# Four plain units instead of eight, another order of the first blocks, and two pairs of heads side by side in a fused retention and PReLU kernel

## The chip, the cores and the metric

The kernel runs on one core of a Trainium2 chip. The metric is the device time of one execution in microseconds (us). The engines are named as in the profile: PE does the matmuls and PEld loads their weights; DVE, ACT and POOL are the vector, scalar and GpSimd engines; SP issues most DMAs, and ACT issues some.

## The reference

Float32 retention over 8 batches, 8 heads, 576 positions and head size 64, followed by a feed-forward layer with a learned PReLU slope:

```python
scores = (1 / sqrt(64)) * q @ k^T
D[i, j] = gamma[h] ** (i - j) if i >= j else 0     # gamma[h] = 1 - 2 ** (-5 - h)
x = ((scores * D) @ v).transpose(0, 2, 1, 3).reshape(4608, 512)
h = x @ w_in                                        # 512 -> 2048
out = (max(h, 0) + alpha * min(h, 0)) @ w_out       # 2048 -> 512
```

The weights arrive in 8-byte floating point, so they are converted on the chip.

## The kernel before

**Retention.** For batches 1 to 7 the unit of work is a pair of heads, numbered `4 * batch + c`; pairs 4 to 7 are batch 1. Each sequence is cut into nine chunks of 64 positions. `load_kq` and `load_v` load a pair: q and k in a layout of 128-byte runs (tiles `qx`, `kx`, eight transfers of 72 KB), k again by rows (`kn`), and v (`vn`). `operands` scales q on POOL and turns `kx` and `qx` on DVE into `kT` and `qT`. `joint(n)` first makes the values of pair n-1 (matmul at line 758), whose copies go to the block tiles `x`; then, for pair n, the scores (L804, L796), the chunks' states (L813), the masked scores in `at`, and a recurrence over the chunks that leaves the running sums in `su`. Two DMAs carry `su` into `vn` and two carry `qT` into `at`, so the values are one product per chunk. For pairs 4 to 7 (`FIRST`) the masks run on ACT and POOL instead of DVE, and part of the loads is issued by ACT. Batch 0 is computed by position instead, in three parts of 256, 256 and 64 positions for all heads (`load_part`, `part_transposes`, `part_scores`, `part_states`, `part_values`, `last_part`), so that the first blocks have their x early.

**Feed-forward.** The 4608 positions form 18 blocks of 256, and the 2048 hidden features eight units of 256. A cell is one block with one unit. Blocks 0 and 1 lie in batch 0; block 2 needs batch 0 and batch 1; block 3 needs batch 1; block 4 also needs batch 2. The weights of a unit are four pieces of 128 x 1024 values: two of `w_in` and two of `w_out`. `convert` makes a piece float32 (two steps on ACT, three on DVE, one on POOL); `split_w` splits a piece into three parts of fewer bits (one step each on ACT, POOL and DVE), and `split_x` does it for a block's x.

A *split* unit (`unit`, then `split_g` and `second`) multiplies such parts: 24 matmuls at L1015 and 12 at L1064. A *plain* unit (`unit_plain`, `second_plain`; L951, L981) multiplies in plain float32 and needs only the converted weights and the unsplit x. Before, the first eight cells are plain: block 0 with units 0 and 1, block 1 with units 0 to 3, block 0 with units 2 and 3. All others are split.

**Order of blocks.** `order` lists visits: a block and the units done in it. A visit accumulates its units in PSUM and writes its sum to `o_kept` (or, at the end, to the output); a later visit of the same block loads that sum as `op` and adds to it. Blocks 0 to 13 are visited with units 0 to 3, blocks 14 to 17 in short visits while the other half of the weights replaces the first, then blocks 0 to 13 with units 4 to 7. `fetch_x` writes a block's x to memory at its first visit and reads it back at later ones. `todo` says after which cells the `joint` of a later pair is put, and `ahead` where the late weights are converted.

**PSUM.** There are eight banks: `psh` 2 (first products, values), `pso` 4 (second products), `psa` 2 (scores, states).

**The planner.** The code first records operations with an engine, an assumed cost, and what they read and write. `plan` derives each operation's urgency in a pass from the last operation backward, then fills the engines forward in time, the most urgent ready operation first. The result is a fixed order on each engine. SP and ACT issue DMAs in that order too, and an instruction that must wait holds up all that is behind it on its engine. `dma` (L218 to L220) records a transfer of any kind; all transfers therefore have line L220.

Functions that the change touches, with the profile's line numbers:

Of the kernel before, what the change touches and what calls it, by code (L numbers as in the profile page):

```python
# [21 lines left out]
def kernel(  # L22
# [195 lines left out]
    def dma(to, fro, size, r, w, eng="SP"):  # L218
        queue = {"SP": nc.sync, "ACT": nc.scalar}[eng]
        do(eng, 0.56, lambda: queue.dma_start(to(), fro()), r, w, late=size / RATE)  # L220
# [103 lines left out]
    LAG, FIRST = 2, range(4, 8)  # L324
# [296 lines left out]
    def convert(raw, wa, to, c=None):  # L621
# [33 lines left out]
        if to is None:  # L655
            tg, t0 = a, 0
        else:
            tg, t0 = to
# [4 lines left out]
            op1=ALU.bitwise_or), raws + [ck], [key] + ([ck] if to is None else []), lock=lock)  # L663
# [11 lines left out]
    plain = {}  # L675
# [23 lines left out]

    def load_kq(n):  # L700
        b, c = pairs[n]
        kx, qx, kn = Gen(kxs), Gen(qxs), Gen(kns[n % 2])
        loaded[n] = kx, qx, kn, vnm[n % 2]
        for g, src in ((qx, q), (kx, k)):
            for a in range(4):
                f0 = (a % 2) * 32
                dma(lambda g=g, a=a: g.get().rearrange("p (n r) -> p n r", r=32)[
                        32 * a:32 * a + 32],
                    lambda src=src, a=a, f0=f0: src[b, 2 * c + a // 2].rearrange(
                        "(n t) d -> t n d", t=32)[:, :, f0:f0 + 32], S * P, (), [(g, a)],  # L710
                    "ACT" if n in FIRST and g is qx else "SP")
# [12 lines left out]
    def operands(n):  # L724
# [3 lines left out]
        def f():  # L728
            qh = qx.get().rearrange("p (j x r) -> p j x r", x=2, r=32)
# [3 lines left out]
        four = [(qx, a) for a in range(4)]  # L733
        do("POOL", 1.15, f, (), four, lock=True)
        kT, qT = turned[n] = Gen(kTs[n % 2]), Gen(qTs[n % 2])
        for to, fro in ((kT, kx), (qT, qx)):
            do("DVE", 0.77, lambda to=to, fro=fro: nc.vector.transpose(to.get(), fro.get()),
               [(fro, a) for a in range(4)], [(to, 0)])
# [9 lines left out]
    def values(n, pv):  # L748
# [5 lines left out]
        for i, js in enumerate((range(0, j1), range(j1, NJ))):  # L754
            def f(i=i, js=js):
                for j in js:
                    for h2 in range(2):
                        nc.tensor.matmul(pv[i].get()[half(h2), (j - js[0]) * C:(j - js[0] + 1) * C],  # L758
                                         vns[n % 2][:, h2, j], mt.get()[:, h2, j], start=True,
# [18 lines left out]
    def joint(n):  # L778
# [10 lines left out]
        ps = [Gen(psa[p2]) for p2 in range(2)]  # L789
# [27 lines left out]
        mt = mts[n] = Gen(ats)  # L817
        for h2 in range(2):
            dma(lambda h2=h2: mt.get()[half(h2), h2].rearrange("p j s -> p (j s)"),
                lambda h2=h2: qT.get()[half(h2)], S * D * 4, [(qT, 0)], [(mt, "q", h2)])  # L820

        def masks(p2):
            for h2 in range(2):
                if n in FIRST:
                    def f(h2=h2):
                        to, x, h = half(1 - h2), half((1 - h2, h2)[p2]), 2 * c + h2
                        nc.scalar.activation(mt.get()[to, h2, p2:NJ - 1:2], at(p2)[x, 0],
# [3 lines left out]
                    def f(h2=h2):  # L831
                        t = mt.get()[half(1 - h2), h2, p2:NJ - 1:2]
# [7 lines left out]
        def masked(p2, h2):  # L840
            to, x, h = half(1 - h2), half((1 - h2, h2)[p2]), 2 * c + h2
            nc.vector.scalar_tensor_tensor(  # L842
                out=mt.get()[to, h2, p2:NJ - 1:2], in0=at(p2)[x, 0], scalar=pf[x, 1, h:h + 1],
                in1=mask[x, None, :].to_broadcast([C, NM - 1, C]), op0=ALU.mult, op1=ALU.mult)
        masks(0)
        for h2 in range(2):
            def f(h2=h2):
                to, h = half(1 - h2), 2 * c + h2
                nc.vector.scalar_tensor_tensor(
                    out=mt.get()[to, h2, NJ - 1], in0=pv[1].get()[to, 7 * C:],  # L850
                    scalar=pf[to, 1, h:h + 1], in1=mask[to], op0=ALU.mult, op1=ALU.mult)
            do("DVE", 0.285, f, [(pv[1], "x")], [(mt, "x", h2)])
        su = Gen(sus)
        g1, g2 = gch[:, 0, c:c + 1], gch[:, 1, c:c + 1]
        do("ACT", 0.37, lambda: nc.scalar.copy(su.get()[:, 0::2], at(0)[:, 1]), [(ps[0], 1)],
           [(su, "e")])
        for h2 in range(2):
            def f(h2=h2):
                x, y = half(h2), half(1 - h2)
                nc.vector.scalar_tensor_tensor(  # L860
                    out=at(0)[x, 0], in0=su.get()[x, 0::2], scalar=g1[x], in1=at(1)[y, 1],
# [3 lines left out]
        do("ACT", 0.22, lambda: nc.scalar.copy(su.get()[:, 1], at(0)[:, 0, 0]), [(ps[0], 0)],  # L865
           [(su, 1)])
        for j in range(3, NJ - 1, 2):
            do("DVE", 0.285, lambda j=j: nc.vector.scalar_tensor_tensor(
                out=su.get()[:, j], in0=su.get()[:, j - 2], scalar=g2, in1=at(0)[:, 0, j // 2],
                op0=ALU.mult, op1=ALU.add), [(su, j - 2), (ps[0], 0)], [(su, j)])  # L870
        do("DVE", 0.42, lambda: nc.vector.scalar_tensor_tensor(
            out=su.get()[:, 2::2], in0=su.get()[:, 1:NJ - 3:2], scalar=g1, in1=at(0)[:, 1, 1:],
            op0=ALU.mult, op1=ALU.add), [(su, 1), (su, 3), (su, 5), (ps[0], 1)], [(su, "e")])
        for h2 in range(2):
            dma(lambda h2=h2: vns[n % 2][half(h2), h2, 1:],
                lambda h2=h2: su.get()[half(h2)], (S - C) * D * 4,
# [3 lines left out]
    order = [(0, (0, 1)), (1, (0, 1, 2, 3)), (0, (2, 3))]  # L880
    order += [(kb, (0, 1, 2, 3)) for kb in range(2, 14)]
# [16 lines left out]
    def fetch_x(vis):  # L898
# [5 lines left out]
        else:  # L904
            x = Gen(xs[taken[0] % 2])
# [5 lines left out]
    def split_x(vis):  # L911
        x = vis["from"]
# [55 lines left out]
    def second_plain(cell):  # L968
        vis, u, ga = cell["vis"], cell["u"], cell["ga"]
        kb = vis["kb"]  # L970
        if cell["first"]:
            acc[:] = [Gen(pso[2 * (vis["n"] % 2) + m]) for m in range(2)]
# [123 lines left out]
    spare = Gen(lxs[1])  # L1096
# [4 lines left out]
    def weights(n):  # L1101
        for _ in range(n):
# [3 lines left out]
            elif at in (12, 14):  # L1106
                homes[0] = Gen(gs[at // 2 % 2])
# [162 lines left out]
```

## Time and profile before

| | |
|---|---|
| median of 3 runs (lowest, highest) | 980.65 us (980.06, 981.99) |
| the profiled execution's own time | 980.06 us |
| its span, first to last instruction | 978.3 us |
| mean granted TensorE clock | 0.984 |
| PE busy | 938.9 us, 96% of the span |
| PEld busy | 822.9 us, 84% |
| DVE, ACT, POOL busy | 615.4, 583.8, 638.1 us |
| moved by DMA | 134.93 MB, mean 138 GB/s |
| DMA packets | 255053, of them 218448 under 512 B |

Busy times are unions of the instructions' spans on an engine. Matmuls overlap in a pipeline, so a product's cost is best read from the distance between the starts of two groups. The granted clock is the share of full TensorE speed in a stretch. In a timeline a line gives the start, the duration, the engine, the line of code, the operation, its tiles and a count; in brackets, the idle time before it and what ended that. `SPq` is SP's instruction queue. DMA share is the mean busy share of 16 engines; packets in several queues at a time can bring it above 1.

### The profile page before, as it was taken

Reading aid. Unit: us, or ns where it says so; the run is one execution under the profiler, and the core shown is the slowest. Engines: PE = TensorE matmul, PEld = TensorE weight load, DVE = VectorE, ACT = ScalarE, POOL = GpSimd, SP = SyncE. Lnnn points to the kernel's source line nnn. Section 1 sums busy time; section 2 is a strip of 40 time slices with the busy share of each in tenths; the row PEclk is TensorE's granted clock in tenths of the full one; section 3 lists DMA queues with packets and bytes.
Section 4 is the critical chain, followed back from the end, with each engine's and each line's share of the span. In section 5 each row is a group of like instructions: output and inputs, shape, how many; then the busy total and the mean of one; then the engine's idle time right before and its main releaser. Section 6 shows DMA issues by size and latency. Waiting matters only on the chain.

```text
span 978.3 us, 22758 instructions
## 1 busy us (share of the span) xinstructions
PE 938.9 (96%) x8713; PEld 822.9 (84%) x8713; DVE 615.4 (63%) x1294; ACT 583.8 (60%) x1313; POOL 638.1 (65%) x515
## 2 busy tenths in 40 slices
PE   4897789999999999999999999999999999999998
PEld 3664578888998888888889899999999999999996
DVE  4777766778676777787667777654454445444444
ACT  2574455757666657575677676665555555555542
POOL 3666665766875857567688889765555555665553
PEclk9899889999999999999999999999999999999999
DMA  9989797788775879887533525242222222221111
GB/s 234 201 152 237 145 210 148 200 185 195 183 150 130 204 151 219 185 199 200 175 130 130 172 98 188 95 150 66 65 76 73 90 65 66 65 87 44 44 45 65
DMA packets 255053, 134.93 MB, mean 138 GB/s; under 512 B 218448, under 2 KB 218464, under 8 KB 254944
## 3 DMA queue, kind: packets, MB, share of 16 engines
q1 hardware_dynamic: 238624, 130.59, 52.5%
q10 hardware_dynamic: 16320, 2.89, 2.1%
q8 instruction: 68, 1.11, 0.5%
q14 instruction: 41, 0.34, 0.1%
HBM read 82.19 MB, written 35.65 MB: 120 GB/s over the span
## 4 chain that ended last, share of the span: by engine, by line
PE 85%; DMA 6%; DVE 3%; POOL 2%; issue 2%; ACT 1%; SPq 1%; ACTq 0%; POOLq 0%; DVEq 0%
PE psh L1015 38%; PE pso L1064 36%; PE psh L758 3%; PE psh L951 2%; DMA kn<-in_k_dram 2%; PE psa L804 1%; PE pso L981 1%; PE psa L813 1%; DMA vn<-su 1%; DMA w<-in_q_dram 1%; SPq L220 1%; DMA kx<-in_k_dram 1%; DMA op<-in_moe_w_in_dram 1%; DMA w<-in_moe_w_out_dram 1%; DVE at L842 0%
## 5 line engine op out<-in xcount | busy, mean ns | idle before, releaser
L1015 PEld LDWEIGHTS psh<-lx,w 128*128 128x128 f32 x3264 | 410.6, 192 | 14.0 <-DVE ga L1030 2.0
L1015 PE MATMUL psh<-lx,w 128*128 128x256 f32 x3264 | 420.0, 284 | 0.4 <-DVE ga L1030 0.3
L1064 PE MATMUL pso<-w,g 128*128 128x512 f32 x1632 | 402.8, 393 | 1.0 <-POOL g L1046 1.0
L1064 PEld LDWEIGHTS pso<-w,g 128*128 128x128 f32 x1632 | 295.8, 188 | 57.9 <-POOL g L1046 2.1
L1043 POOL TENSOR_TENSOR g<-ga,g 128x512 fp32r<-128x512 f32 x136 | 180.4, 1327 | 234.0 <-ACT g L1039 233.7
L1024 DVE SCALAR_TENSOR_TENSOR ga<-psh,gt 128x256 f32<-128x256 f32 x272 | 114.6, 422 | 175.8 <-ACT gt L1023 170.3
L1046 POOL TENSOR_TENSOR g<-g 128x512 fp32r<-128x512 f32 x136 | 178.5, 1312 | 12.0 <-ACT g L1041 2.0
L1030 DVE SCALAR_TENSOR_TENSOR ga<-psh,malpha,ga 128x256 f32<-128x256 f32 x272 | 130.2, 480 | 67.9 <-ACT psh L1027 66.9
L1027 ACT ACTIVATE psh<-ga 128x256 f32<-128x256 f32 x272 | 105.2, 388 | 88.3 <-DVE ga L1024 87.3
L1039 ACT ACTIVATE g<-ga 128x512 fp32r<-128x512 f32 x136 | 85.8, 631 | 119.8 <-PE pso L1064 105.9
L1023 ACT COPY gt<-psh 128x256 f32<-128x256 f32 x272 | 101.0, 371 | 67.6 <-PE psh L1015 59.6
L934 POOL TENSOR_TENSOR lx<-lx 128x512 fp32r<-128x512 f32 x78 | 102.4, 1322 | 18.8 <-DVE lx L924 16.2
L1041 ACT ACTIVATE g<-ga 128x512 fp32r<-128x512 f32 x136 | 84.3, 620 | 0.0
L842 DVE SCALAR_TENSOR_TENSOR at<-psa,pf,mask 64x256 f32<-64x256 f32 x96 | 46.3, 483 | 18.1 <-PE psh L758 7.0
L758 PEld LDWEIGHTS psh<-at,vn 128*64 128x64 f32 x1008 | 34.8, 143 | 18.9 <-issue 11.5
L758 PE MATMUL psh<-at,vn 128*64 128x64 f32 x1008 | 39.9, 232 | 9.3 <-DMA kx<-in_k_dram 6.8
L917 ACT ACTIVATE lx<-x 128x512 fp32r<-128x512 f32 x78 | 48.7, 628 | 0.0
L730 POOL TENSOR_TENSOR qx<-qx,tabx 128x576 f32<-128x576 f32 x28 | 32.6, 1166 | 23.9 <-DMA qx<-in_q_dram 17.9
L931 POOL TENSOR_TENSOR lx<-x,lx 128x512 fp32r<-128x512 f32 x30 | 38.8, 1292 | 3.2 <-ACT lx L929 3.2
L1082 DVE TENSOR_TENSOR op<-pso,op 128x512 f32<-128x512 f32 x46 | 31.5, 686 | 14.2 <-PE pso L1064 14.2
L773 ACT COPY x<-psh 128x256 f32<-128x256 f32 (+3 forms) x84 | 23.7, 321 | 18.2 <-PE psh L758 12.5
L924 DVE TENSOR_TENSOR lx<-x,psa 128x512 fp32r<-128x512 f32 x48 | 32.6, 679 | 2.1 <-PE psh L1015 1.9
(173 smaller groups left out, 848.9 us busy)
## 6 DMA issues: line engine op xcount, KB each, us to landing
ok<-o SPq DMA_DIRECT2D x48, 256.0 KB, 2.9
op<-ok SPq DMA_DIRECT2D x24, 512.0 KB, 4.0
x<-xk SPq DMA_DIRECT2D x23, 512.0 KB, 3.4
xk<-x SPq DMA_DIRECT2D x18, 512.0 KB, 4.7
out_dram<-o SPq DMA_DIRECT2D x36, 256.0 KB, 2.1
kx<-in_k_dram SPq DMA_DIRECT2D x112, 72.0 KB, 3.3
vn<-in_v_dram SPq DMA_DIRECT2D x56, 144.0 KB, 3.4
at<-qT SPq DMA_DIRECT2D x56, 144.0 KB, 3.0
```

Source lines behind the costliest of these rows:

```text
L758: nc.tensor.matmul(pv[i].get()[half(h2), (j - js[0]) * C:(j - js[0] + 1) * C], vns[n % 2][:, h2, j], mt.get()[:, h2, j], start=True, stop= ...
L934: do("POOL", 1.29, lambda c=c: nc.gpsimd.tensor_tensor(out=piece(to.get()[:, 2, c]), in0=to.get()[:, 0, c], in1=to.get()[:, 1, c], op=ALU. ...
L1015: nc.tensor.matmul(at(b), piece(w[:, l, c0:c0 + P]), piece(x.get()[:, l, cc]), start=(n == 0 and cc == 0), stop=(n > 0 and cc == NCC - 1), ...
L1023: do("ACT", 0.36, lambda t=t, at=at: nc.scalar.copy(t(), at(1)), [(ph, 1)], [(gt, f)])
L1024: do("DVE", 0.42, lambda t=t, g=g, at=at: nc.vector.scalar_tensor_tensor(out=g(), in0=at(0), scalar=ONE, in1=t(), op0=ALU.mult, op1=ALU.su ...
L1027: do("ACT", 0.39, lambda g=g, at=at: nc.scalar.activation(at(1), g(), ACTF.Relu, scale=-1.0), [(ga, f)], [(ph, 1)])
L1030: do("DVE", 0.48, lambda g=g, at=at, fc=fc: nc.vector.scalar_tensor_tensor(out=g(), in0=at(1), scalar=malpha[:, fc:fc + 1], in1=g(), op0=A ...
L1039: do("ACT", 0.64, lambda: nc.scalar.mul(piece(to.get()[:, 2]), ga.get(), BELOW), both, [(to, 2)])
L1041: do("ACT", 0.64, lambda: nc.scalar.mul(piece(to.get()[:, 0]), ga.get(), BELOW * 2.0 ** -12), both, [(to, 0)])
L1043: do("POOL", 1.29, lambda: nc.gpsimd.tensor_tensor(out=piece(to.get()[:, 1]), in0=ga.get(), in1=to.get()[:, 2], op=ALU.subtract), both + [ ...
L1046: do("POOL", 1.29, lambda: nc.gpsimd.tensor_tensor(out=piece(to.get()[:, 2]), in0=to.get()[:, 0], in1=to.get()[:, 1], op=ALU.subtract), [( ...
L1064: nc.tensor.matmul(a[2 * m + b].get(), piece(g.get()[:, l, f, m * P:(m + 1) * P]), piece(w_at[u, 2 + f].get()[:, l]), start=(cell["first"] ...
```

## The change

1. **Plain units.** Only four cells are plain: blocks 0 and 1, each with units 0 and 1. The former plain cells with units 2 and 3 become split cells.
2. **Visits.** Blocks 0 to 3 are visited in the order 0 (units 0, 1), 1 (0, 1), 2 (0, 1), 3 (0 to 3), 2 (2, 3), 1 (2, 3), 0 (2, 3): seven visits in place of five. The first split cell is block 2 with unit 0. `todo` and `ahead` are moved accordingly. Blocks 4 and up keep their order.
3. **Two pairs at once.** Pairs 5 and 7 (`APART`) keep their `kx`, `qx`, masked scores and running sums in one of the two buffers of the split x (`lx0`), and their scores and states in the PSUM banks `pso2` and `pso3`. Pairs 4 and 5, then 6 and 7, can thus run beside each other. Plain second products use only `pso0` and `pso1`.
4. **Weights.** Pieces 0 to 7 are converted into `lx1` and `g0`; pieces 8 to 15 are converted in their own raw buffers (`HERE`), with the intermediate words in SBUF, not PSUM. Pieces 0 to 7 are split between pairs 5 and 6 in the recorded order, pieces 8 to 11 after pair 8, and 12 to 15 one by one behind their conversions. Before, all sixteen splits were recorded after the last plain cell.
5. **Reuse of a split x.** If the visit before the last was of the same block (three such cases), its split x is used again: no read and no split.
6. **Bytes in flight.** For transfers that the plan starts before 100 us, an SP transfer waits for the landing of an earlier one: going back from itself over the transfers of both queues, the one before which the sizes have reached 5 x 262144 bytes (1.31 MB).

The diff's core:

```diff
     def dma(to, fro, size, r, w, eng="SP"):
-        queue = {"SP": nc.sync, "ACT": nc.scalar}[eng]
-        do(eng, 0.56, lambda: queue.dma_start(to(), fro()), r, w, late=size / RATE)
+        def f():
+            ins = {"SP": nc.sync, "ACT": nc.scalar}[eng].dma_start(to(), fro())
+            if now[0] < LIMITED:
+                ahead = size
+                for other, n in reversed(flight):
+                    if eng == "SP" and ahead >= IN_FLIGHT:
+                        tc.add_manual_dep(ins.ins, other.ins.name, mybir.DependencyInfo(
+                            mybir.DependencyClass.Sync, mybir.DependencyReason.DATA),
+                            reason="bytes in flight")
+                        break
+                    ahead += n
+                flight.append((ins, size))
+        do(eng, 0.56, f, r, w, late=size / RATE)
+
+    flight, now = [], [0.0]
+    LIMITED, IN_FLIGHT = 100.0, 5 << 18
...
-    LAG, FIRST = 2, range(4, 8)
+    LAG, FIRST, APART = 2, range(4, 8), (5, 7)
...
+    def apart():
+        if not aside:
+            g = Gen(lxs[0])
+            aside.append(g)
...
+            g.kx, g.qx, mt, su = at(0, S), at(S, 2 * S), at(2 * S, 4 * S), at(4 * S, 4 * S + 8 * D)
...
     def load_kq(n):
         b, c = pairs[n]
-        kx, qx, kn = Gen(kxs), Gen(qxs), Gen(kns[n % 2])
+        if n in APART:
+            kx, qx, kn = apart(), apart(), Gen(kns[n % 2])
+        else:
+            kx, qx, kn = Gen(kxs), Gen(qxs), Gen(kns[n % 2])
+            kx.kx, qx.qx = kx.get, qx.get
...
-        ps = [Gen(psa[p2]) for p2 in range(2)]
+        ps = [Gen(b) for b in ((pso[2], pso[3]) if n in APART else psa)]
...
-        mt = mts[n] = Gen(ats)
+        if n in APART:
+            mt = su = apart()
+        else:
+            mt, su = Gen(ats), Gen(sus)
+            mt.mt, su.su = mt.get, su.get
+        mts[n] = mt
...
-    order = [(0, (0, 1)), (1, (0, 1, 2, 3)), (0, (2, 3))]
-    order += [(kb, (0, 1, 2, 3)) for kb in range(2, 14)]
+    order = [(0, (0, 1)), (1, (0, 1)), (2, (0, 1)), (3, (0, 1, 2, 3)), (2, (2, 3)), (1, (2, 3)),
+             (0, (2, 3))]
+    order += [(kb, (0, 1, 2, 3)) for kb in range(4, 14)]
...
-            x = Gen(xs[taken[0] % 2])
+            x = Gen(xs[taken[0] % 2 + (2 if vis["n"] < 7 else 0)])
...
     def split_x(vis):
+        if vis["n"] > 3 and visits[vis["n"] - 2]["kb"] == vis["kb"]:
+            vis["x"] = visits[vis["n"] - 2]["x"]
+            return
...
-            acc[:] = [Gen(pso[2 * (vis["n"] % 2) + m]) for m in range(2)]
+            acc[:] = [Gen(pso[m]) for m in range(2)]
...
     def weights(n):
         for _ in range(n):
             at = npiece[0]
-            if at % 6 == 0 and at < 12:
-                homes[0] = Gen(lxs[at // 6])
-            elif at in (12, 14):
-                homes[0] = Gen(gs[at // 2 % 2])
-            convert(*next(raws), (homes[0], DM * (at % 6 if at < 12 else at % 2)), psa[1])
+            if at in (0, 6):
+                homes[0] = Gen((lxs[1], gs[0])[at // 6])
+            convert(*next(raws), (homes[0], DM * (at % 6)) if at < 8 else HERE,
+                    psa[1] if at < 8 else None)
...
     part_scale(2, 1)
     part_scale(2, 2)
     second_plain(cells[1])
-    unit_plain(cells[2])
     last_part()
     operands(NPAIR)
     load_kq(NPAIR + 1)
     load_v(NPAIR + 1)
-    weights(2)
+    joint_(4)
+    unit_plain(cells[2])
+    joint_(5)
+    for i in range(8):
+        split_w(i)
     second_plain(cells[2])
     unit_plain(cells[3])
...
-    ahead = {10 + 3 * i: 1 for i in range(16)}
+    ahead = {18 + 14 * i // 5: 1 for i in range(16)}
...
-    for cell in cells[8:]:
+    for cell in cells[4:]:
...
     for op in best[1]:
+        now[0] = best[2][op.n]
         op.fn()
```

## The prediction

> **What bounds the kernel now.** I read the page's tenths first, then busy time by stretch, then the PE and SP timelines around the first split unit.
>
> The page, busy tenths in 40 slices of 24.5 us; granted clock and DMA share below:
> ```profile
> PE   4897789999999999999999999999999999999998
> ...
> PEclk9899889999999999999999999999999999999999
> DMA  9989797788775879887533525242222222221111
> ```
> PE is full from the seventh slice to the end; all that can be saved beside PE's own work lies in the first 150 us, where DMA is the full resource. By stretch (PE, PEld, DVE, ACT, POOL busy us; then clock, DMA share, GB/s):
> ```profile
> 0.00:60.00 60.00, 42.97 (x741) 32.57 (x742) 39.86 (x99) 29.37 (x49) 34.98 (x44) 0.89 1.02 208
> 60.00:91.00 31.00, 26.37 (x282) 15.88 (x279) 21.96 (x41) 17.54 (x35) 18.68 (x18) 0.95 0.98 199
> 91.00:123.00 32.00, 24.18 (x264) 17.30 (x262) 22.94 (x42) 15.13 (x32) 22.25 (x21) 0.89 0.83 165
> 123.00:140.00 17.00, 13.87 (x244) 10.87 (x244) 10.00 (x22) 9.92 (x24) 13.92 (x12) 0.88 0.87 200
> ...
> 180.00:978.30 798.30, 791.61 (x6720) 710.93 (x6720) 491.51 (x1023) 490.20 (x1120) 530.93 (x409) 1.00 0.47 126
> ```
> To 140 us PE idles 32.6 of the span's 39.4 us. DMA moves about 200 GB/s to 91 us and only 165 from 91 to 123: there the attention chain of batch 1, one pair of heads after the other, sets the pace. PE's timeline at the end of that chain:
> ```profile
> 123.03 1.27 PE L758 MATMUL psh<-at,vn 128*64 128x64 f32 x36
> ...
> 128.56 3.71 PE L1015 MATMUL psh<-lx,w 128*128 128x256 f32 x24
> ...
> 137.07 2.32 PE L758 MATMUL psh<-at,vn 128*64 128x64 f32 x32 [1.31 <-DMA vn<-su]
> 139.38 4.59 PE L1015 MATMUL psh<-lx,w 128*128 128x256 f32 x24
> ```
> At 123.03 pair 7, the last of batch 1, gets its values; 5.5 us later (copies, split of x) the first split unit starts; the second waits for 139.38. The running sums that release the values go out on SP (start, duration):
> ```profile
> 72.61 1.17 SPq L220 DMA_DIRECT2D vn<-su  x2
> ...
> 90.56 1.15 SPq L220 DMA_DIRECT2D vn<-su  x2
> ...
> 105.38 1.15 SPq L220 DMA_DIRECT2D vn<-su  x2
> ...
> 119.50 1.15 SPq L220 DMA_DIRECT2D vn<-su  x2
> ```
> Pairs 4 to 7: 18, 15 and 14 us apart.
>
> **The change, part by part.**
>
> Fewer plain units. A plain unit's first product takes 3.66 us (chain: L951 x16 from 68.30), its second 3.53 (L981 x8, 119.50 to 123.03), 7.2 in all. A split unit takes 5.62 (L1015 groups start at 950.69 and 956.31). Four plain ones turned into split ones save 4 x 1.6 = 6.3 us of PE work. But those four were PE's cover in the loading phase: 29 us of work leave it and come back as 22.5 us behind it. So what decides is how much earlier the first split unit can start. Call its start t1.
>
> What is left at t1. Before, from the second split unit (139.38) to the end are 838.9 us, stalls and tail included. At t1 the changed order has left the same plus four split units (22.5), plus one unit's first product (2.87), pair 9's states (0.6) and pair 8's values (1.2), which the order of PE's instructions puts behind t1: 838.9 + 22.5 + 4.7 = 866.1. **Span = t1 + 866.1**, if the later stalls stay as they are. Break-even is t1 = 112.2.
>
> t1 from the DMA side. In the changed SP and ACT orders I counted what is issued up to pair 7's running sums: q, k, v of batch 0 (3.5 MB), twelve weight pieces instead of sixteen (6.3), k, v, q copies and sums of batch 1 and early loads of batch 2: 18.9 MB, 48 of them transfers of 72 KB in 128-byte runs (kx, qx). Before, 18.6 MB had moved at 91 us, with 32 such transfers, and 23.9 MB at 123 us. The small ones are dear: four kx loads hold SP for 8.5 us from 62.98, beside qx loads on ACT, so some 0.9 us each where the same bytes in bulk take 0.3. Sixteen more of them: 16 x 0.6 = 10 us. Pair 7's sums land at 91 if the small ones hide beside bulk, at 101 if not.
>
> t1 from the chain's side. Two pairs run side by side, so pair 6 follows pair 4 and pair 7 follows pair 5: sums land (3.4), values (1.3), v loads (4.2), states (0.65), copy and recurrences (0.37 + 1.02 + 0.21 + 0.84 + 0.41): 12.4 us, 14.5 with hand-offs and the sibling's share of PE and DVE. Pair 5's sums stand behind 14.5 MB with 37 small transfers; 14.2 MB had moved at 70 us before, so about 79 us with the extra small ones and the landing; plus 14.5 is 94. Between 94 (chain) and 101 (DMA), nearer to DMA, since the queue also carries batch 2: I take 100. With the measured 0.5 us to PE and 5.5 us from values to unit, **t1 = 106**.
>
> Other engines up to t1. By the order, POOL has about 53 us of work there (8 conversions and 8 splits at 1.3, masks 16 x 0.73, scales, x), DVE 60, ACT 72 with issues: none is the bound, though POOL has the split of x last (4 x 1.28), which is in the 5.5.
>
> The other edits. Pairs 5 and 7 in a split-x buffer and two spare accumulators: no instruction added; cost 0 while plain units use two banks only; a plain evacuation (0.6) is the worst, covered before t1. Conversions of pieces 8 to 15 in place: DVE's steps go from PSUM to SBUF, same count; bounds -3 to +3 us on DVE, off the path. Splits of weights early: 16 x 1.3 on POOL remain; only eight must precede t1; this is what lets t1 come before the last pieces land. Pieces 12 to 15 are issued within 6.7 MB after pair 7's sums, landing by 130; unit 3 of block 3 needs them near 131 for its first and 148 for its second product: 0, at worst 5 us. Two more short visits: x reloads, o_kept writes and one or two op loads, 2.6 MB, some 10 us of DMA in a stretch (150 to 180) where DMA was 0.70 busy: covered. POOL from t1 to block 4 has 48 operations, some 62 us, in 71 us of PE: covered, 0 to 4 us. Reused splits of x take as many away later as the new visits add. From block 4 on the orders agree but for the timing of conversions: 0, -1 to +2.
>
> Bytes in flight. About twenty SP transfers before 100 us get a second wait, on an older transfer's landing. Behind each stand SP's later loads and the chain's own q copies and sums. 1.31 MB at 208 GB/s is 6.3 us of transfer; transfers landed 4.8 to 8 us after issue, so DMA should seldom run dry. Bounds: -3 us (k and q of batch 0, which took 7.9 us to land beside v, come sooner) to +13 (each wait empties DMA 0.65 us). I take 0, as the queue before is held by landings too: its waits for qx, w and kn loads sum to 24 us up to 140 us.
>
> A rule against the change. PE's granted clock was 0.50 from 20 to 30 us after a stall and 0.87 from 140 to 150; the latter's 1.3 us are within 838.9. With less cover PE idles more. The Trainium skill ("TensorE: Matmul & The Clock Gate", Part 1: The HAM clock gate) says an idle window of about 3.4 us halves the clock and as much sustained work restores it; by that, an estimate, three more restarts behind t1 would cost 3 x 1.7 = 5 us, and the time would be 980. By the row it is one restart, as before. I keep the row.
>
> Sum: 106 + 866.1 = 972.1 span. The profiled execution's own time was 980.06 for 978.3, so 1.8 lies around it, and the median is 0.6 above: **974.5**.
>
> **The rivals.**
>
> *Early* (0.22): DMA stays as full as from 10 to 40 us (share 1.14 to 1.18, 191 to 287 GB/s), and the chain bounds. Sums at 94, t1 = 100, time 968.5; with first loads 3 us sooner, 965. For: DMA dips to 0.75 from 70 to 80 for want of ready transfers. Against: small transfers.
>
> *Given back at block 4* (0.17): block 4 needs batch 2, whose bytes before it are not fewer. Before, pair 11's values ran at 179.91 and block 4 at 188.45. With t1 = 106 block 4 is due at 182, so those values at 174; the 2.6 MB more could hold them at 180. The gain of 6 us shrinks to 0 to 2: 979 to 981.
>
> *Slower* (0.20): the byte limit starves the queue. Each of the twenty waits holds up a chain transfer on the same in-order queue; at 0.65 us or more each, sums land at 113, t1 = 119, span 985, time 987.5. It decides from t1 = 112, 0.3 us a wait. Against: 6.3 us of bytes stay in flight.
>
> That the change does not do its work is excluded: the instruction orders show four plain units and two interleaved pairs.
>
> **How the numbers follow.** Forecast (t1 103 to 109, 971.5 to 977.5) 0.41. Faster by over 0.2% (below 978.7; about what a measurement of this kernel can tell from no change): 0.41 + 0.22 + 0.03 of the block-4 case = 0.66. Within: 0.11 of that case. Slower: its remaining 0.03 and 0.20. The range, 961 to 988, leaves out the ends of the early and the slower case.
>
> **What would show it.** Right: the last batch-1 sums (vn<-) land near 100, first split unit at 103 to 109, 140 split units at 5.6 us, PE idle of some 40 us, nearly all before 110. Wrong: first split unit after 112; PE stalls of several us between it and block 4's first unit (due near 182); DMA share below 0.9 from 40 to 100 us with SP waiting for old landings.

## The result, and the profile after

The changed kernel takes 989.31 us (median of 4 runs, 988.26 to 990.94) against 980.36 (978.37 to 981.99) for the kernel before on the same chip: ratio 1.0094, 95% interval 1.0069 to 1.0119. It is slower, by some 9 us; 974.5 had been forecast, and the time lies just above the range. The profiled execution took 988.26 us, its span is 986.5, its mean granted clock 0.979 (before: 980.06, 978.3, 0.984).

The page of the changed kernel, busy tenths in 40 slices of 24.7 us, with clock and DMA share:

```profile
PE   4796699999999999999999999999999999999997
...
PEclk9888699999999999999999999999999999999999
DMA  9998888777775888778543544242122221221112
```

PE is full from the sixth slice on, one earlier than before, but the fifth (99 to 123 us) has fallen to 6, at a clock of 0.6. By stretch (PE, PEld, DVE, ACT, POOL busy us; clock, DMA share, GB/s), the last row from block 4's first unit to the end:

```profile
0.00:60.00 60.00, 40.10 (x799) 31.64 (x800) 40.27 (x97) 28.77 (x49) 39.28 (x48) 0.86 1.04 193
60.00:91.00 31.00, 25.15 (x324) 15.70 (x322) 20.35 (x42) 18.17 (x39) 15.45 (x19) 0.94 0.90 193
91.00:112.00 21.00, 10.24 (x205) 8.35 (x204) 16.51 (x31) 10.52 (x25) 15.19 (x13) 0.60 0.82 185
112.00:150.00 38.00, 36.34 (x375) 32.40 (x368) 32.56 (x64) 26.70 (x63) 28.96 (x23) 0.95 0.89 216
150.00:190.00 40.00, 39.73 (x425) 35.58 (x426) 29.67 (x66) 28.55 (x66) 37.99 (x30) 1.00 0.82 198
189.98:986.50 796.52, 785.87 (x6645) 704.89 (x6643) 492.57 (x1010) 477.19 (x1090) 515.01 (x398) 1.00 0.46 124
```

The same last stretch of the kernel before, from its block 4 at 188.45 to its end:

```profile
188.45:978.30 789.85, 783.71 (x6618) 704.06 (x6612) 484.91 (x1006) 482.56 (x1102) 524.21 (x404) 1.00 0.47 126
```

One group of scores (32 matmuls, some 0.6 us) stands just ahead of block 4 in the kernel before, and behind block 4's start in the changed one:

```profile
187.83 0.69 PE L804 MATMUL psa<-qT,kT 64*64 64x64 f32 x32 [0.54 <-DVE su L871]
```

So the 8.2 us of span come in two parts. **Up to block 4** the changed kernel is 1.5 us later (189.98 for 188.45), although it has 6.9 us less work there (6.3 by the forecast's prices for the plain units, and these scores). PE's busy time up to that point fell by only 3.6 us (from 155.2, the page's total less the row above), and its idle time rose from 33.3 to 38.4 us. **From block 4 on** it takes 6.7 us more for the same matmuls and those scores: 4.5 of idle time and 2.2 of longer busy time, all at clock 1.00.

The first split unit does start 16.5 us earlier, as intended. PE's timeline around it:

```profile
96.51 2.38 PE L788 MATMUL psh<-at,vn 128*64 128x64 f32 x32 [2.28 <-DMA vn<-su]
...
102.51 2.31 PE L788 MATMUL psh<-lx,vn 128*64 128x64 f32 x30 [0.21 <-DMA vn<-lx]
104.75 0.47 PE L843 MATMUL psa<-vn,kn 64*64 64x64 f32 x2
106.76 1.12 PE L843 MATMUL psa<-vn,kn 64*64 64x64 f32 x30 [1.54 <-DMA vn<-in_v_dram]
111.00 1.13 PE L834 MATMUL psa<-qT,kT 64*64 64x64 f32 x32 [3.12 <-DVE su L905]
112.06 4.80 PE L1053 MATMUL psh<-lx,w 128*128 128x256 f32 x24
...
120.53 3.13 PE L1053 MATMUL psh<-lx,w 128*128 128x256 f32 x24 [0.26 <-ACT x L803]
```

Everything here is slow: values take 2.3 us where they took 1.27 before, states and scores 1.1 where they take 0.69 at full clock, the first split unit's first product 4.80 where the second's takes 3.13. And on PE the unit stands behind pair 9's scores (111.00), which waited 3.12 us for DVE. The running sums of pairs 4 to 7 go out on SP (start, duration):

```profile
74.93 1.11 SPq L220 DMA_DIRECT2D vn<-su  x2
...
76.84 1.10 SPq L220 DMA_DIRECT2D vn<-lx  x2
...
93.71 1.29 SPq L220 DMA_DIRECT2D vn<-su  x2
...
99.51 1.11 SPq L220 DMA_DIRECT2D vn<-lx  x2
```

They go in two couples, 2 and 6 us apart, where before each pair was 14 to 18 us behind the last; but from pair 4 to 6 it is 18.8 us and from 5 to 7 it is 22.7, not 14.5.

### The profile page after: what moved, and what is told of

Its sections match the earlier page's. It is cut to its first block, busy times and chain, and to the rows that moved or that the text cites. A ratio compares the mean times of both kernels' runs of the same rounds, so it can differ in the third digit from the quotient of the medians.

```text
span 986.5 us, 22943 instructions
## 1 busy us (share of the span) xinstructions
PE 937.4 (95%) x8761; PEld 828.5 (84%) x8761; DVE 631.9 (64%) x1306; ACT 589.9 (60%) x1329; POOL 651.9 (66%) x525
## 3 DMA queue, kind: packets, MB, share of 16 engines
q8 instruction: 69, 1.13, 0.5%
## 4 chain that ended last, share of the span: by engine, by line
PE 80%; DMA 7%; DVE 4%; SPq 3%; ACT 2%; issue 2%; POOL 1%; ACTq 1%; POOLq 0%; DVEq 0%
PE psh L1053 37%; PE pso L1102 35%; SPq L220 3%; PE psh L788 2%; DMA kn<-in_k_dram 1%; PE psh L989 1%; DMA qx<-in_q_dram 1%; PE psa L843 1%; PE psa L834 1%; DMA vn<-in_v_dram 1%; DMA w<-in_moe_w_in_dram 1%; DMA op<-in_moe_w_out_dram 1%; DMA x<-in_moe_w_out_dram 1%; DVE ga L1068 1%; DMA op<-in_moe_w_in_dram 1%
## 5 line engine op out<-in xcount | busy, mean ns | idle before, releaser
L1053 PEld LDWEIGHTS psh<-lx,w 128*128 128x128 f32 x3360 | 423.1, 192 | 21.1 <-DVE ga L1068 7.8
L1053 PE MATMUL psh<-lx,w 128*128 128x256 f32 x3360 | 433.9, 284 | 5.5 <-DVE ga L1068 4.4
L1102 PE MATMUL pso<-w,g 128*128 128x512 f32 x1680 | 413.8, 393 | 0.6 <-POOL g L1084 0.3
L1102 PEld LDWEIGHTS pso<-w,g 128*128 128x128 f32 x1680 | 304.8, 188 | 58.8 <-POOL g L1084 0.8
L1081 POOL TENSOR_TENSOR g<-ga,g 128x512 fp32r<-128x512 f32 x140 | 186.2, 1330 | 223.7 <-ACT g L1077 223.4
L1084 POOL TENSOR_TENSOR g<-g 128x512 fp32r<-128x512 f32 x140 | 183.5, 1311 | 11.3 <-ACT g L1079 0.9
L1065 ACT ACTIVATE psh<-ga 128x256 f32<-128x256 f32 x280 | 108.4, 388 | 99.7 <-DVE ga L1062 98.5
L1077 ACT ACTIVATE g<-ga 128x512 fp32r<-128x512 f32 x140 | 88.3, 631 | 121.3 <-PE pso L1102 107.1
L972 POOL TENSOR_TENSOR lx<-lx 128x512 fp32r<-128x512 f32 x76 | 97.9, 1298 | 19.0 <-DVE lx L962 16.6
L1079 ACT ACTIVATE g<-ga 128x512 fp32r<-128x512 f32 x140 | 86.7, 619 | 0.0
L969 POOL TENSOR_TENSOR lx<-x,lx 128x512 fp32r<-128x512 f32 x34 | 44.7, 1313 | 4.7 <-DMA at<-qT 3.4
L1125 DVE SCALAR_TENSOR_TENSOR o<-pso,op 128x512 f32<-128x512 f32 x52 | 35.8, 688 | 1.1
```

What stands on the lines that cost most here:

```text
L972: do("POOL", 1.29, lambda c=c: nc.gpsimd.tensor_tensor(out=piece(to.get()[:, 2, c]), in0=to.get()[:, 0, c], in1=to.get()[:, 1, c], op=ALU. ...
L1053: nc.tensor.matmul(at(b), piece(w[:, l, c0:c0 + P]), piece(x.get()[:, l, cc]), start=(n == 0 and cc == 0), stop=(n > 0 and cc == NCC - 1), ...
L1065: do("ACT", 0.39, lambda g=g, at=at: nc.scalar.activation(at(1), g(), ACTF.Relu, scale=-1.0), [(ga, f)], [(ph, 1)])
L1077: do("ACT", 0.64, lambda: nc.scalar.mul(piece(to.get()[:, 2]), ga.get(), BELOW), both, [(to, 2)])
L1079: do("ACT", 0.64, lambda: nc.scalar.mul(piece(to.get()[:, 0]), ga.get(), BELOW * 2.0 ** -12), both, [(to, 0)])
L1081: do("POOL", 1.29, lambda: nc.gpsimd.tensor_tensor(out=piece(to.get()[:, 1]), in0=ga.get(), in1=to.get()[:, 2], op=ALU.subtract), both + [ ...
```

## The experiments

In all of them t1 is the start of the first split unit, "block 4" the start of block 4's first unit, and "from block 4" the span from there to the end. Ratios are to the kernel before, on the same chip in the same session.

**1 and 2. The limit on bytes in flight**, taken from the changed kernel (a_nolimit) and put alone into the kernel before (b_limit). The edit of a_nolimit:

```diff
-    LIMITED, IN_FLIGHT = 100.0, 5 << 18
+    LIMITED, IN_FLIGHT = 0.0, 5 << 18
```

> The changed kernel without the limit on bytes in flight (the bound in planned time set to 0; the order on every engine is the same). Theory L, the limit starves the chain: pair 4's sums, ready at 67.7 us but issued at 74.9 behind a landing, go out within 2 us of being ready, the first split unit starts 5 to 8 us before 112.1 and the time falls by 5 to 8 us, to 981 to 984. Theory C, the lost cover (idle PE, half clock, instructions in order behind late loads): the limit costs under 2 us, the time stays at 987 to 991 and the first split unit within 2 us of 112.

> The kernel before with the limit on bytes in flight alone. Theory L: slower than before by 4 us or more, with SP waiting longer for landings up to 100 us. Theory C: within 2 us of before.

Measured: a_nolimit 988.82 us, ratio 1.0069 (1.0045 to 1.0093), t1 113.52, block 4 at 191.21. b_limit 980.98 us, ratio 0.9992 (0.9974 to 1.001). The limit costs nothing that can be measured in either kernel. Pair 4's sums, which DVE has ready at 67.7, leave SP at 74.9 with the limit and without it. In the chain of waits the release follows a load of `kn` that ACT issued and that lands after 6.3 us; the sums read nothing of it, and why SP waits for it is not shown. In the same order with long runs in the q and k loads (5) pair 4's sums leave at 68.6, so that the wait hangs on those loads in some way.

**3. One chain.** The changed kernel with no pair set apart.

```diff
-    LAG, FIRST, APART = 2, range(4, 8), (5, 7)
+    LAG, FIRST, APART = 2, range(4, 8), ()
```

> The changed kernel without pairs 5 and 7 beside 4 and 6 (one chain of pairs, as before); all else stays, and the planner orders anew. If the two chains earn what the prediction gave them, the sums of pair 7 land 10 to 20 us later than 102.5 and the time is 997 to 1010. If the chain's length does not decide, because the queue of loads does, within 4 us of 989.

Measured: 999.29 us, ratio 1.0173 (1.0149 to 1.0198); sums at 68, 81, 95 and 109 us, t1 124.84, block 4 at 200.2. Two chains earn 10 us, all of them ahead of block 4 (from there on it takes 796.3). The other edits together lose more than that: this kernel is 17 us slower than the one before, and up to block 4 its PE is idle for 50.6 us where it was 33.3 before. That the missing cover is the main part of this is argued, not shown.

**4. Where the late conversions are put.** The kernel before with the changed kernel's `ahead`.

```diff
-    ahead = {10 + 3 * i: 1 for i in range(16)}
+    ahead = {18 + 14 * i // 5: 1 for i in range(16)}
```

> The kernel before with the changed placing of the sixteen late weight conversions (cells 18 to 60 instead of 10 to 55); the planner orders anew. From block 4 on the changed kernel lost 6.4 us more than before. If the placing of the conversions costs that, this kernel is 4 to 7 us slower than before, with PE waiting for DVE between 200 and 620 us. If the loss has another source, it stays within 2 us of before.

Measured: 980.95 us, ratio 0.9996 (0.9978 to 1.0013); from block 4 791.4 us. The placing alone does not bring the loss.

**5. Long runs in the small loads.** The q and k loads of pairs 4 to 9 read runs of 2304 bytes in place of 128, the same bytes in number; the heads of these pairs then are not what the reference computes.

```diff
...
+                        src[b, 2 * c + a // 2].rearrange(
+                        "(t n) d -> t (n d)", t=32)[:, 18 * f0:18 * f0 + S].rearrange(
+                        "t (n d) -> t n d", d=32)
...
```

> The changed kernel, but the q and k loads of pairs 4 to 9 in the small layout read runs of 2304 bytes instead of 128 (the same bytes per transfer, wrong places, so batch 1 and a part of batch 2 are not what the reference computes); the order is the same. If the small runs fill the queue and thereby set the first split unit, the sums of pair 7 land 8 us or more before 102.5, the first split unit starts near 103 and the time falls by 8 us or more, to 981 or less. If the chain of dependent steps sets it (12.4 us of steps and the hand-offs), the unit comes at most 4 us earlier and the time is 984 or more.

Measured: 986.55 us, ratio 1.0021 (1.0002 to 1.0041, in a session where the kernel before ran at 983.18); t1 111.29, 0.8 us earlier; pair 7's sums at 98.9 in place of 99.5. The short runs, which the forecast had charged with 10 us, hardly set t1. They did hold the sums of pairs 4 and 5, which left at 68.6 and 72.4 in place of 74.9 and 76.8; this lead was gone before pair 6's (93.6 for 93.7). The ratio is 0.7% lower than the changed kernel's, with intervals apart; where the time is won is not shown, as the profiled execution (988.84) was the slowest of ten.

**6. A dearer price for them in the plan.** The planner is told three times their size.

```diff
-                        "(n t) d -> t n d", t=32)[:, :, f0:f0 + 32], S * P, (), [(g, x, a)],
+                        "(n t) d -> t n d", t=32)[:, :, f0:f0 + 32], 3 * S * P, (), [(g, x, a)],
```

> The changed kernel with the planner told a threefold size for each q and k load in 128-byte runs; what is moved stays. If the order went wrong because small loads are planned too cheap, the sums wait less behind them and the time falls by 4 us or more, to 985 or less. If not, the new order gives 985 to 994.

Measured: 1050.11 us, ratio 1.0679 (1.0637 to 1.0721). t1 came 4 us earlier, at 108.4, but block 4 only at 205.1, and from there it took 841.9 us with 36 us of idle time. The price holds for all batches, and the whole plan is another: no answer on the loads.

**7. Pair 9's loads later.** Pair 9 belongs to batch 2, yet its loads lie ahead of pair 7's sums.

```diff
+        if x == 8:
+            load_kq(9)
...
-        if x + 2 < len(pairs):
+        if x + 2 < len(pairs) and x + 2 != 9:
```

> The changed kernel with the q and k loads of pair 9 recorded after pair 8's joint step instead of before it, so that they no longer lie ahead of pair 7's sums on SP. If the queue ahead of the sums costs 5 us, the first split unit comes at 107 or before and the time is 983 to 986; if the chain behind pair 5 decides, within 3 us of 989.

Measured: 988.84 us (984.84 to 994.64), ratio 1.0065 (1.0037 to 1.0093); in the profiled execution, of 986.38 us, t1 is 104.95, 7.1 us earlier than in the changed kernel and 1 us better than the forecast had it; block 4 is at 187.75, only 2.2 earlier; from block 4 796.9 us. The plan changed in more than pair 9's loads: pair 4's sums leave at 66.4 and pair 7's at 95.5, and the weight splits that DVE did at 93 to 101 us in the changed kernel come from 103.7 on. PE's timeline shows the first part of the loss:

```profile
104.95 1.65 PE L1053 MATMUL psh<-lx,w 128*128 128x256 f32 x6
108.88 4.09 PE L1053 MATMUL psh<-lx,w 128*128 128x256 f32 x18 [2.28 <-POOL lx L972]
...
115.78 3.14 PE L1053 MATMUL psh<-lx,w 128*128 128x256 f32 x24
```

The first unit starts with a quarter of its x and waits 2.28 us for POOL's split of the rest; the 18 matmuls that follow run at half clock. The second unit is 4.7 us earlier than in the changed kernel, not 7.1, and five stalls of 0.3 to 0.6 us on the way to block 4 (2.3 in all, for 0.6 in the changed kernel) take 1.7 more.

**8. A filler that keeps the clock up.** Ten groups of four identity products, into a free bank, ahead of pair 7's values.

```diff
+    for _ in range(10):
+        hot = Gen(pso[3])
+
+        def fill(hot=hot):
+            for i in range(4):
+                nc.tensor.matmul(hot.get()[:, i * P:(i + 1) * P], ident, ident, start=True,
+                                 stop=True)
+        do("PE", 0.5, fill, (), [(hot, 0)])
```

> The changed kernel with ten times four idle matmuls (identity by identity into a free bank, read by nobody) recorded ahead of pair 8's joint step; the planner puts them before pair 7's values. If the half clock behind the idle stretch costs what the trace shows (values 2.3 instead of 1.2, states 1.1 instead of 0.65, first split unit 4.8 instead of 3.0 us), those run at full speed and the time falls by 2 to 4 us, unless the new order loses it elsewhere. If the clock is not on the path, the time stays within 2 us of 989 while the three durations shrink.

Measured: 997.35 us, ratio 1.0138 (1.0102 to 1.0174); t1 112.92, block 4 at 196.7. The trace has them between 97 and 111 us, most of them 8.45 us at a stretch. PE's timeline behind them:

```profile
110.33 1.27 PE L788 MATMUL psh<-lx,vn 128*64 128x64 f32 x36
111.53 0.69 PE L834 MATMUL psa<-qT,kT 64*64 64x64 f32 x32
112.92 0.50 PE L1053 MATMUL psh<-lx,w 128*128 128x256 f32 x2 [0.70 <-ACT lx L955]
...
117.70 4.12 PE L1053 MATMUL psh<-lx,w 128*128 128x256 f32 x18 [1.79 <-POOL lx L972]
```

The filler did warm what it was put before: values 1.27 us for 2.31, scores 0.69 for 1.13. But it stood in PE's way (pair 7's values came at 110.3 in place of 102.5), and the split x came piecemeal, so that the unit fell back to half clock. A waiting PE kept busy is worth about 1.5 us on these two steps and cost more than that; how much of the rest is the new plan is not shown.

**9 and 10. The reuse of a split x**, taken from the changed kernel and put alone into the kernel before (where it holds for the three late visits; in the changed kernel it holds for four, block 2's second visit being the fourth, not for three as the text above has it).

```diff
+        if vis["n"] > 3 and visits[vis["n"] - 2]["kb"] == vis["kb"]:
+            vis["x"] = visits[vis["n"] - 2]["x"]
+            return
...
```

> The changed kernel without the reuse of a split x: the four visits that took over the split x of the visit before the last (block 2's second visit and three of the late short visits) read x again and split it again, as the kernel before did. Theory R (the reuse shifts the visits' work on POOL, DVE and the weight splits of blocks 14 to 17, and that is the loss behind block 4): from block 4's first unit to the end 790 to 792 us, the stretch from block 14 to the 72nd unit from the end 92.9 us, time 983 to 985. Theory P (the loss behind block 4 is a matter of how the list scheduler happens to lay the later instructions, whatever edit moves them): that stretch stays at 795 to 798 us, time 988 to 991. Theory S (the reuse saves what it takes away): 990 to 992.

> The kernel before with the reuse of a split x alone (three late short visits). Theory R: from block 4 on 794 to 797 us in place of 790, time 983 to 987. Theory P: within 1.5 us of the kernel before, or a shift with no pattern in those visits. Theory S: 0.5 to 1 us faster.

Measured: a_noreuse 990.91 us, ratio 1.0106 (1.0079 to 1.0132), from block 4 801.4 us (in an execution of 997.33 us, the slowest of six). b_reuse 985.85 us, ratio 1.0046 (1.0028 to 1.0065), from block 4 794.5. Without the reuse the changed kernel is no faster (the intervals overlap), and with it the kernel before is slower. The first is against theory R; what suggests itself is that any edit which makes the scheduler plan anew moves the time by some us.

**11 to 16. Other plans of the same work.** The planner's assumed DMA rate, 220 GB/s, is set to 219, 221 and 222 in both kernels. Nothing else is changed; instructions are the same, their order is another.

```diff
-    RATE = 220e3
+    RATE = 221e3
```

> The changed kernel with the planner's assumed DMA rate at 221 in place of 220 GB/s: nothing else is changed, so that its plan is another draw of the same scheduler. Theory P: t1 within 3 us of 112, and from block 4 on anything from 790 to 799 us, time 985 to 994. Theory R, or any cause by structure: from block 4 on 795 to 798, time 988 to 991.

> The kernel before with the planner's assumed DMA rate at 221 in place of 220 GB/s. Theory P: from block 4 on 789 to 797 us, time 978 to 987. A cause by structure: 790 to 792 as in all three plans of the kernel before that have run, time 979 to 982.

> The changed kernel with the planner's assumed DMA rate at 219 in place of 220 GB/s: another plan of the same work. Theory P (the loss behind block 4 is the draw of the plan): from block 4 to the end somewhere from 790 to 800 us, overlapping the plans of the kernel before (790 to 794 so far). Theory Q (the changed kernel has a loss of its own there): 795 to 800 us, never below 795, time 987 to 994.

> The changed kernel with the planner's assumed DMA rate at 222 GB/s, as above. Theory P: from block 4 on 790 to 800 us. Theory Q: 795 to 800 us, time 987 to 994. Either way t1 within 3 us of 112 and block 4 at 188 to 192.

> The kernel before with the planner's assumed DMA rate at 219 GB/s. Theory P: from block 4 on 790 to 798 us, time 980 to 990. Theory Q: at most 794 us, time 980 to 986.

> The kernel before with the planner's assumed DMA rate at 222 GB/s. Theory P: from block 4 on 790 to 798 us, time 980 to 990. Theory Q: at most 794 us, time 980 to 986.

Measured (us; the three columns on the right from each kernel's profiled execution):

| kernel, rate | median | ratio (interval) | t1 | block 4 | from block 4 |
|---|---|---|---|---|---|
| before, 220 | 980.36 | 1 | 128.6 | 188.5 | 789.9 |
| before, 219 | 985.30 | 1.0037 (1.0022 to 1.0052) | 131.4 | 191.5 | 792.0 |
| before, 221 | 986.38 | 1.0055 (1.0035 to 1.0075) | 127.5 | 187.8 | 793.8 |
| before, 222 | 993.34 | 1.0126 (1.0084 to 1.0168) | 132.1 | 188.3 | 805.3 |
| changed, 220 | 989.31 | 1.0094 (1.0069 to 1.0119) | 112.1 | 190.0 | 796.5 |
| changed, 219 | 988.05 | 1.0075 (1.0059 to 1.009) | 116.1 | 191.7 | 793.9 |
| changed, 221 | 992.91 | 1.0115 (1.0097 to 1.0134) | 111.3 | 191.0 | 800.2 |
| changed, 222 | 987.05 | 1.0065 (1.0049 to 1.0081) | 111.2 | 189.3 | 797.8 |

Theory Q falls on both of its conditions: a changed plan lies below 795 us from block 4 on (by 1.1 us), and a plan of the kernel before lies above 794, above all of the changed ones even. Each figure in the three columns on the right is from one execution, and executions of one plan differ by 2 to 8 us in their whole time; at rate 221 the profiled one of the kernel before was the fastest of five, 3 us below the median. What is to be seen:

- From block 4 on, the plans of the kernel before spread over 15 us and those of the changed kernel over 6, and they overlap. The 6.7 us there are within what the draw of a plan makes; 790 is the best of eight plans. That a few of them are the change's own is not excluded: with the other experiments that planned anew (4 and 10; 3, 7, 8 and 9), five of six plans of the kernel before take 789.9 to 794.5 us, and eight of the changed kernel 793.9 to 801.4.
- Up to block 4 the plans agree. Block 4 starts at 189.0 us before and 190.5 after, in the mean of four, although t1 is 15 to 21 us earlier at the same rate. Up to there the change does nothing to the good.
- The four medians have means of 986.3 and 989.3 us. With spreads of 13 and 6, four plans do not tell these apart.

What the loss looks like is seen in the matmuls' waits from block 4 on (busy us, mean ns of one; idle before them and what ended it). The first products of the changed kernel, then of the kernel before, then of the kernel before at rate 222:

```profile
L1053 PE MATMUL psh<-lx,w 128*128 128x256 f32 x3072 | 394.6, 284 | 4.6 <-DVE ga L1068 3.8 <-ACT x L803 0.7
```

```profile
L1015 PE MATMUL psh<-lx,w 128*128 128x256 f32 x3072 | 392.8, 283 | 0.3 <-DVE ga L1030 0.3
```

```profile
L1015 PE MATMUL psh<-lx,w 128*128 128x256 f32 x3072 | 396.0, 284 | 5.0 <-ACT x L773 1.9 <-DVE ga L1030 1.3 <-POOL lx L934 1.1
```

It is the same kind of loss in both kernels: a first product that waits some half us for the evacuation of an earlier one (`ga`) or for a copy of attention values. One stall of the same kind in the changed kernel, here before a pair's values, all engines, in order of time:

```profile
222.14 0.78 ACT L772 ACTIVATE kn<-kn,tabk 128x576 f32<-128x576 f32 x1 [2.50 <-DMA kn<-in_k_dram]
...
222.82 0.36 ACT L1061 COPY gt<-psh 128x256 f32<-128x256 f32 x1
...
223.21 0.42 DVE L1062 SCALAR_TENSOR_TENSOR ga<-psh,gt 128x256 f32<-128x256 f32 x1 [2.95 <-ACT gt L1061]
...
224.08 1.41 PE L788 MATMUL psh<-at,vn 128*64 128x64 f32 x36 [0.67 <-DVE ga L1068]
```

ACT stood 2.5 us at the scaling of a later pair's `kn`, whose load landed late; behind it in ACT's order was the evacuation, behind that DVE's step, and behind that PE's next user of the bank. So an order that was planned for a transfer that lands in time can cost PE time when it does not. That this holds for the other stalls was not traced.

## Why the prediction was wrong

The forecast was span = t1 + 866.1 with t1 = 106. Measured: t1 = 112.06, and 874.5 behind it. The 14.4 us by which the span is longer than forecast are, rounded, 6.1 up to t1, 1.7 from there to block 4 (77.9 for 76.2) and 6.7 from block 4 on.

**The end of the chain: nearly right, for another reason.** Pair 7's sums were to land at 100 us; they left SP at 99.5, and its values ran from 102.5. But the reason given was DMA with its small transfers, and with long runs (5) they left at 98.9. Nearer is the chain of dependent steps: its spacing was put at 14.5 us and came to 18.8 and 22.7. What the forecast's sum of that chain left out is other work that the fixed orders put between its steps:

```profile
79.55 4.78 PE L989 MATMUL psh<-x,lx 128*128 128x256 f32 x16
...
90.98 3.76 POOL L675 TENSOR_TENSOR w<-w 128x512 int32<-128x512 int32 x3
...
93.05 3.47 DVE L703 SCALAR_TENSOR_TENSOR w<-w,w 128x512 fp32r<-128x512 f32 x1
...
94.71 1.25 POOL L700 TENSOR_TENSOR w<-w,w 128x512 fp32r<-128x512 f32 x1
...
96.55 1.02 DVE L894 SCALAR_TENSOR_TENSOR pso<-lx,gch,pso 64x256 f32<-64x256 f32 x2
```

Pair 5's sums had landed at 79.8, but a plain unit's first product stood ahead of its values on PE, which came at 84.26. And pair 7's recurrence (L894) stood behind a weight split on DVE (L703) that took 3.47 us where its median is 0.69; the last section has more on that. That "none is the bound" was true of DVE's and POOL's sums of work, not of their order. The recurrence ended at 99.45; but SP issued pair 9's loads until 98.6, so that the DVE step by itself held the sums for less than 1 us. With another plan (7), where neither stood there, the sums left at 95.5. No run took one of these away alone.

**From values to unit: the step that made t1 late.** The forecast took the measured 5.5 us from the kernel before. It was 9.55 us from 102.51: 1 us because values run at half clock; 0.5 more in the copies and the split of x up to the third of POOL's four steps, at whose end the unit had started before (128.4) and which ends at 109.5 here; 2.5 because pair 9's scores, waiting for DVE until 111.00, stand ahead of the unit on PE. Together with values that were 2 us late (102.5 for 100.5) this is the 6 us. I had carried over a distance that was measured at full clock and with nothing of another pair between values and unit on PE to a place where neither held.

**The clock: right behind t1, left out ahead of it.** Three stretches of the changed kernel:

```profile
90.00:100.00 10.00, 5.17 (x103) 3.60 (x101) 9.69 (x17) 4.41 (x12) 7.69 (x8) 0.77 0.77 149
100.00:110.00 10.00, 5.08 (x72) 3.96 (x72) 6.96 (x14) 4.96 (x13) 6.43 (x6) 0.50 0.79 217
110.00:120.00 10.00, 7.96 (x126) 7.40 (x128) 6.89 (x10) 6.21 (x15) 7.81 (x6) 0.71 1.04 212
```

From 95.4 to 115.9 us the clock stayed at half, 20.5 us without a break; the kernel before had five half-speed stretches of 3.4 to 10.2 us, the changed one four of 3.4 to 20.5. Half of PE's busy time in these stretches, an estimate of what they cost, is 11.5 us before and 15.0 after up to block 4. Behind t1 "one restart, as before" held: 3.8 us at half clock, to 115.9, where the kernel before has 3.3 behind 139.38, a loss of 1.9 for 1.6, so that the first split unit's 4.80 us stand for the 4.59 which the 838.9 contain. The 1.7 us between t1 and block 4 are mostly waits, 1.9 us for 0.7. What the forecast put at nothing is the clock ahead of t1, where it slowed the chain itself: values by 1 us, states and scores by 0.4 each. The Trainium skill ("TensorE: Matmul & The Clock Gate", Part 1: The HAM clock gate) has the clock halve after an idle window of about 3.4 us and return after as much sustained work. The forecast's estimate from it, 5 us, was for restarts behind t1, and these did not come. And the trace shows what the rule as I read it does not: just before 95.4 no gap was that long. One of 1.45 us had ended at 93.3 and one of 2.28 us was half over; gaps of 0.2 to 3.1 us followed while the clock stayed down.

**The saving: right in size, spent before block 4.** Four plain units less are worth 6.3 us. PE's busy time up to block 4 fell by 3.6, which is these 6.3 and the 0.6 of the scores, less 3.5 of clock, to 0.2. Idle time up to block 4 rose by 5.1, of which none lies behind t1: up to 112 us PE is idle 36.5 us (112 less the first three rows) where it was 29.5 before, from there to 190 it is 1.9 for 3.8. The cover that the plain units gave was worth about as much as the units cost. "So what decides is how much earlier the first split unit can start" was the right question, with the break-even at t1 = 112.2 and t1 at 112.06.

**Given back at block 4: not as it was priced.** That rival had pair 11's values hold block 4 at 188. Block 4 did start at 190, but from 121 us to it PE waited less than a us in all (68.35 of 68.98 us busy); it was full of work. Only where t1 came earlier (7) was a part of the head start lost on the way, to the wait for x and to small waits, 4.9 of 7.1 us.

**Slower, by the byte limit: wrong mechanism.** Its time (987.5) is near the measured one by chance. The limit costs nothing that can be measured (1 and 2), as the forecast's own term had it.

**From block 4 on: the second step that failed.** "From block 4 on the orders agree but for the timing of conversions: 0, -1 to +2" was 6.7 us. I had taken equal work in a like order for equal time. Eight plans show a spread of 15 us for work that is the same. The kernel before stands on the best of its four plans, and a change that makes the planner start anew can lose that: from block 4 on the other three take 7 us more in the mean, 5.5 with the plans of (4) and (10). So this term should have been some +6 with bounds from 0 to +15, and the forecast with it near 980 even at t1 = 106. Which of the plan's choices makes a given stall was read in one case only, above, and whether a part of the 6.7 us is the change's own stays open. Of the 2.2 us of longer busy time there 0.6 are the scores that moved; most of the rest lies in the first products (394.6 us for 392.8), the group that waits.

No version tried beats the kernel before.

## What to carry to other kernels

Where a planner fixes the order of thousands of instructions, a few reruns with one of its constants nudged (here 1 GB/s in 220) tell how much of a gain or loss the plan alone can make; do that before a cause is sought, and put the spread into every forecast that touches the recorded work. Work that covers a loading phase was worth about its own length here: what is moved out of it has to be paid for by an earlier end of the chain behind it, and the milestone to price is the first point where both kernels have the same work left, here block 4, not the first unit of the new kind. A distance between two milestones carries over only with the clock and the order of work that it was measured with, and a chain of steps is only as short as the other work that its engines' orders put between them.

## What was not expected of the hardware

- Half clock after short gaps: two gaps of 1.45 and 2.28 us lay within 4.7 us, and inside the second the clock fell to 0.50, where it stayed for 20.5 us although PE was busy for 12.4 of them. At 460 us of the changed kernel at rate 221 a single stall of 2.62 us came with 6.8 us of half clock, in the midst of full work.
- In all 18 traces the half-speed stretches inside the span last whole multiples of 3.41 us: 3.4, 6.8, 10.2, 17.1, 20.5 and so on.
- A DVE step on two inputs in SBUF (L672, 128 x 512) has a median of 0.69 us and a longest of 1.77, from 200 to 640 us. In one such case, 1.65 us from 225.79 to 227.44, POOL ran a step on two inputs until 226.89, 0.55 us before DVE's end. The Trainium skill ("SBUF — State Buffer", SBUF: two separate sides) says that DVE and GpSimd share a port pair that one of them holds for a whole instruction, and the trace agrees. It is not one instruction only: the split of 3.47 us above began at 93.05, outlasted three POOL steps and ended at 96.52, again 0.55 us behind the last of them (95.97). In the 18 traces some 270 such conversion and split steps took over 1.5 us, the longest 6.08 (rate 221), and every one ended 0.55 to 0.56 us behind the end of a POOL step.
